# One batch's last transform stage with its products apart, and other steps for folds, stages and mixes in a fused FFT and channel-mix kernel

## The chip, the cores and the metric

The kernel runs on one core of one Trainium2 chip. The metric is the device time of an execution in microseconds. The kernel before the change took 428.42 us (median of 3 runs, 428.34 to 428.61).

The engines named below: PE multiplies matrices, ACT applies functions and copies, DVE does elementwise work, POOL issues the loads (and a few small operations), SP issues the stores. PE writes to PSUM alone, so each product is copied out by ACT or DVE ("evicted") before its PSUM buffer can be used again.

## The reference

```
# x: (8, 3072, 256); mu_k, mu_r: (256,); w_k: (256, 1024); w_v: (1024, 256); w_r: (256, 256)
X = np.fft.fft(x, axis=1)
X = np.fft.fft(X, axis=2)
x = X.real                                   # the mixed tokens

x_prev = concat([zeros, x[:, :-1, :]], axis=1)
xk = mu_k * x + (1.0 - mu_k) * x_prev
xr = mu_r * x + (1.0 - mu_r) * x_prev
k = np.maximum(xk @ w_k, 0.0)
v = k * k @ w_v
r = 1.0 / (1.0 + np.exp(-(xr @ w_r)))
out = r * v
```

First the real part of a two-dimensional Fourier transform over the sequence and the features of each batch, then a channel mix: a token shift with two weightings, a product with `w_k`, the square of its positive part, a product with `w_v`, and a gate.

## The kernel before, in words

**The channel mix sets the clock.** Each of the 8 batches has 6 chunks of 512 tokens (`m` says which half of the spectrum, `i` which third), 48 chunks in all, and each chunk has 4 steps. One step of the main loop does a K part (`k_piece`: 4 matmuls of 512 columns for two of the eight blocks of the hidden width, then the positive part on ACT into `rl`) and a v part (`v_tile`: 8 matmuls of 256 columns into a psV buffer, 5 steps behind the K part, `LAG`). Every fourth step has an r part (`r_item`: 8 matmuls, then a sigmoid on ACT). DVE squares `rl` into `k` two steps' worth at a time at odd steps (`square`, L845), and multiplies v by r into `o` at even steps (`v_out`, L888), which SP stores.

**The transform of later batches runs in between.** For batch `t` it goes through:

1. the load of two halves, plain (`xp`) and mirrored by an indirect gather (`xm`): `load_xh`, issued by POOL, behind `load_gate`, a tiny DVE write that POOL waits for, so that loads start at a chosen place in DVE's order;
2. `fold` (DVE, two adds) for each half, then `butterfly` (batches 1 and 2) or `quarters_1` and `quarters_2` (batch 3 on), all on DVE, into `eo`;
3. stage A: `a_item` or `a_half` (16 small matmuls per half and parity, evicted by ACT into `a`), with `a_slots_0` for two extra columns;
4. stage D: `d_item` (batches 1, 2) or `d_half` (from batch 3) into `g_all`, and `turned`, a matmul that fixes one column of `g_all` and writes it back;
5. the last stage, C, over 28 slots. `c_item` accumulates the cosine and the sine product in PSUM: two matmuls of 128 columns per slot, evicted straight into `y`. `c_pairs` keeps the two products apart: two matmuls of 64 columns per slot, evicted into `pq`, and DVE then adds and subtracts them into `y` (`halves`, L759, after one sign change at L756). The change finds batches 0 and 1 with `c_item` and the rest with `c_pairs`;
6. `diff` (DVE: differences of neighbouring slots, the token shift) and `mix(b, j, m, a)` (DVE, a scaling L779 and an add or subtract L790 into `x`). `j` is 0 for the K parts' operand and 1 for the r parts', `m` the half of the spectrum, `a` one of two operand halves. A matmul of a K part reads one `a`.

**What sets the order.** The order is written out by hand: `at(step, f, ...)` puts an item into a step, `event(step, ...)` groups several matmul items of the transform. In a step PE gets the K part, then the items of kind x, then the v part, then the event; DVE gets the x items' part, the event's, then the items of kind w and the product `o`, and last the square (in six steps named in `OUT_FIRST`, `o` comes ahead of the items). If the next step is in `early_v`, its v part follows directly behind the event. `event` puts the next step into `early_v` by itself where it has over two items and the first isn't `a_slots_0`. Every engine works through its own list in order.

**Buffers.** PSUM has three psW buffers in rotation, for K, r and all transform products, and two psV buffers. `p`, `t`, `y`, `pq`, `a`, `g_all`, `d` and each `x` exist once; `eo` twice; `xp` and `xm` three times.

**Batch and step.** Batch `b` has its K parts in steps 24b to 24b + 23. A batch's transform ends just before, so its steps are counted from s = 24t - 48 below.

The loop and the two order functions are in the part printed here; the lines that a sentence can't say:

```
for step in range(nk + LAG):
    if step < nk: k_piece(chunks[step // 4], step % 4)
    due(step, "x")
    v = v_steps.get(step)
    if v and step not in early_v: v_tile(*v)
    ...
    due(step, "e")
    if step + 1 in early_v:
        if step + 1 in v_steps: v_tile(*v_steps[step + 1])
    ...
    due(step, "w")
```

Of the kernel before, what the change touches and what calls it, by code (L numbers as in the profile page):

```python
# [39 lines left out]
def kernel(  # L40
# [12 lines left out]
    B, S, D = x.shape  # L53
# [52 lines left out]
    V = nc.vector  # L106
# [850 lines left out]
    for a in range(2):  # L957
        t = x_t["t", a] = mix_pool.tile([P, 24, 64], FP16, name=f"t{a}")
# [25 lines left out]
    def at(step, f, *args):  # L984
        work.setdefault((step, "x" if f in (a_item, a_sum, d_item, d_small, c_item, c_tiles, turned, minus_0, r_item, quarter_tables) else "w"),
                        []).append((f, args))
# [3 lines left out]
    early_v = set(range(17, 20))  # L990

    def event(step, *items):
        work.setdefault((step, "e"), []).extend((f[0], f[1:]) for f in items)
        if len(items) > 2 and items[0][0] is not a_slots_0:
            early_v.add(step + 1)

    chunks = [(b, m, i) for b in range(B) for m in range(2) for i in range(3)]
    nk = 4 * len(chunks)

    LAG, EARLY, SHORT = 5, 3, 3  # L1000
    EVENTS = (29, 33, 41, 45)
    OUT_FIRST = (12, 20, 28, 36, 38, 40)
    SQUARE_A = (6, 7, 8, 9)
    v_steps = {4 * n + tb + LAG: (c, tb) for n, c in enumerate(chunks) for tb in range(4)
# [23 lines left out]
    at(1, d_small, 0, 12, 1, "V")  # L1028
    at(2, mix_part, 0, 1, 0, 8)
    event(3, (half_tables,))  # L1030
    event(4, (c_item, 0, 17, 8))
    at(1, loads_1)
    at(4, loads_2)
# [26 lines left out]
    at(15, d_item, 1, 1, "V")  # L1060
    at(16, d_item, 1, 2, "A")
    at(16, d_item, 1, 3, "V")
    at(17, turned, 0, 13)
    at(17, r_item, (0, 1, 0))
    at(17, minus_0)
    at(17, c_tiles, 1)
    at(17, fold, 2, 0)
    event(18, (c_item, 1, 0, 8), (c_item, 1, 8, 8))
    at(18, butterfly, 2, 0)
    at(18, fold, 2, 1)  # L1070
    event(20, (c_item, 1, 16, 8), (c_item, 1, 24, 4), (a_half, 2, 0, 0))
    at(19, diff, 1, 0, 12)
    at(20, r_item, (0, 1, 1))
    at(23, a_half, 2, 0, 1)
    at(20, mix, 1, 0, 0, 0, 0, 12)
    at(21, butterfly, 2, 1)
    at(21, mix, 1, 0, 0, 1, 0, 12)
    at(22, diff, 1, 12, 26)
    at(21, load_gate)
    at(21, load_xh, 3, 1)  # L1080
    at(23, mix, 1, 0, 0, 0, 12, 24)
    at(24, r_item, (0, 1, 2))
    at(24, mix, 1, 1, 0, 0)
    at(24, mix, 1, 0, 0, 1, 12, 24)
    at(25, mix, 1, 1, 0, 1)
    at(26, mix, 1, 0, 1, 0)
    event(27, (a_slots_0, 2), (a_half, 2, 1, 0), (a_half, 2, 1, 1))
    at(28, r_item, (1, 0, 0))
    at(28, d_item, 2, 0)
    at(28, mix, 1, 0, 1, 1)  # L1090
    at(29, d_item, 2, 1)
    at(30, mix, 1, 1, 1, 0)
    at(31, d_item, 2, 2)
    at(31, mix, 1, 1, 1, 1)
    at(32, r_item, (1, 0, 1))
    at(33, d_item, 2, 3)
    at(34, turned, 0, 13)
    at(42, quarter_tables)
    for n, c in enumerate(chunks[8:]):
        at(4 * n + 36, r_item, c)  # L1100
    for b in range(B):
        s0 = 24 * b

        for n, st0 in enumerate((2, 4, 6, 8) if b > 1 else ()):
            at(s0 + st0, mix, b, n // 2, 1, n % 2)
        if b and b + 3 < B:
            at(s0 + 22, load_gate)
            for h in range(2):
                at(s0 + 22, load_xh, b + 3, h)
        t = b + 2  # L1110
        if t < B:
            if b:
                at(s0 + 9, fold, t, 0)
                at(s0 + 10, quarters_1, t, 0)
                at(s0 + 11, quarters_2, t, 0)
                at(s0 + 12, fold, t, 1)
                at(s0 + 14, quarters_1, t, 1)
                at(s0 + 15, quarters_2, t, 1)
            c = [(c_pairs, t, 8 * n, (8, 8, 8, 4)[n], "A") for n in range(4)]
            d = [(d_half, t, n) for n in range(4)]  # L1120
            a = [(a_half, t + 1, h, e) for h in range(2) for e in range(2)] if t + 1 < B else []
            if not b:
                event(s0 + 37, *c[:2], a[0])
                event(s0 + 41, *c[2:], a[1])
                event(s0 + 45, (a_slots_0, t + 1), *a[2:])
                continue
            at(s0 + 32, turned, 0, 12)
            at(s0 + 37, turned, 12, 13)
            event(s0 + EVENTS[0], *d[:3])
            early_v.add(s0 + EVENTS[0] + 2)  # L1130
            event(s0 + EVENTS[1], d[3], *c[:2])
            event(s0 + EVENTS[2], *c[2:], *a[:1])
            if a:
                event(s0 + EVENTS[3], (a_slots_0, t + 1), a[2], a[3], a[1])
                early_v.add(s0 + EVENTS[3] + 1)
        t = b + 1
        if b and t < B:
            at(s0 + 16, halves, t, 0, 15)
            at(s0 + 18, halves, t, 15, 27)
            for a in range(2):  # L1140
                at(s0 + 19 + a, diff, t, 0, 26, (a,))
                at(s0 + 21 + a, mix, t, 0, 0, a)
            at(s0 + 24, mix, t, 1, 0, 0)
            at(s0 + 25, mix, t, 1, 0, 1)

    def due(step, kind):
        for f, args in work.pop((step, kind), ()):
# [59 lines left out]
```

## Time and profile before

| | |
|---|---|
| median of 3 runs | 428.42 us |
| the profiled execution, whole | 428.89 us |
| its span, first to last instruction | 427.1 us |
| granted PE clock, mean over the span | 0.999 |
| DVE squares (L845, 2048 columns) | 88 of 1.22 us |
| ACT positive parts (L835) | 192 of 1.03 us |
| loads, issue to landing | 4.6 to 8.4 us |

The profile has views by engine, by line, of waits, of the chain of work that ended last, and a timeline. A timeline's row begins with the start and the length of a group in us; "x8" counts its instructions, and a bracket at the end gives idle time of the engine before it and what ended that. Matmuls overlap, so the time that a group of them takes is read from the start of the group to the start of the next, and not from its length.

### The profile page before, as it was taken

What the parts mean: (1) busy time and instruction counts of PE and PEld (TensorE: products, weight loads), DVE (VectorE), ACT (ScalarE), POOL (GpSimd) and SP (SyncE); (2) the same over time, 40 slices, a digit from 0 to 9 for tenths busy, and PEclk for the clock granted to TensorE, in tenths of its full rate; (3) what the DMA queues carried; (4) which work ended last, traced back from release to release, by engine and by line L of the source; (5) the groups of instructions that cost most, each with busy time, mean ns of one, the idle gap of its engine ahead of it and who ended that gap; (6) DMA issues with size and microseconds to landing.
All of it is one profiled execution on the core that took longest, in us unless ns stands there. A gap on an engine that the chain in (4) does not pass through costs nothing.

```text
span 427.1 us, 9641 instructions
## 1 busy us (share of the span) xinstructions
PE 421.1 (99%) x3991; PEld 295.3 (69%) x3991; DVE 367.8 (86%) x584; ACT 328.6 (77%) x409; POOL 62.3 (15%) x99
## 2 busy tenths in 40 slices
PE   8999999999999999999999999999999999999996
PEld 3767776777667777776777677767767776766765
DVE  8899999999897999979989899989999756997453
ACT  7889897878878878687786967778686877666661
POOL 7378502000050002300040000500000000000000
PEclk9999999999999999999999999999999999999999
DMA  8779967322286224932368222862232322323233
GB/s 172 108 108 188 231 142 131 75 56 69 61 151 157 55 58 82 194 86 57 79 116 179 67 58 67 144 152 61 64 75 51 75 68 58 73 63 71 66 75 99
DMA packets 35104, 42.08 MB, mean 99 GB/s; under 512 B 4114, under 2 KB 31092, under 8 KB 35060
## 3 DMA queue, kind: packets, MB, share of 16 engines
q1 hardware_dynamic: 27488, 25.41, 24.5%
q0 software_dynamic: 7264, 15.80, 22.1%
q8 instruction: 31, 0.51, 0.5%
q10 hardware_dynamic: 308, 0.26, 0.2%
q14 instruction: 13, 0.11, 0.1%
HBM read 32.08 MB, written 25.17 MB: 134 GB/s over the span
## 4 chain that ended last, share of the span: by engine, by line
PE 97%; ACT 1%; DVE 1%; issue 0%; POOL 0%; POOLq 0%
PE psW L825 39%; PE psV L866 37%; PE psW L852 10%; PE psV L878 3%; PE psW L746 1%; PE psW L617 1%; PE psW L235 1%; PE psW L679 1%; PE psW L635 1%; PE psW L657 1%; PE psW L714 1%; PE psV L378 1%; ACT pq L574 0%; DVE rw L308 0%; PE psV L657 0%
## 5 line engine op out<-in xcount | busy, mean ns | idle before, releaser
L835 ACT ACTIVATE rl<-psW 128x1024 f16<-128x1024 f32 x192 | 193.8, 1032 | 82.0 <-PE psW L825 77.1
L825 PE MATMUL psW<-x,wk 128*128 128x512 f16 (+1 forms) x776 | 193.6, 377 | 0.4 <-DVE x L962 0.3
L866 PE MATMUL psV<-wv_sb,k 128*128 128x256 f16 x1424 | 184.2, 273 | 0.0
L866 PEld LDWEIGHTS <-k 128*128 128x128 f16 x1424 | 136.5, 98 | 38.4
L845 DVE TENSOR_TENSOR k<-rl 128x2048 f16<-128x2048 f16 (+1 forms) x100 | 115.5, 1156 | 35.1 <-ACT rl L835 34.7
L825 PEld LDWEIGHTS <-wk 128*128 128x128 f16 x776 | 75.3, 98 | 55.1 <-issue 0.7
L888 DVE SCALAR_TENSOR_TENSOR o<-psV,r 128x512 f32<-128x512 f32 (+1 forms) x97 | 65.7, 680 | 12.2 <-PE psV L866 11.4
L790 DVE TENSOR_TENSOR x<-y,t 128x1536 f16<-128x1536 f16 (+3 forms) x74 | 62.0, 845 | 2.1
L857 ACT ACTIVATE r<-psW 128x1024 f16<-128x1024 f32 x48 | 49.5, 1032 | 0.8 <-PE psW L852 0.8
L852 PE MATMUL psW<-wr,x 128*128 128x256 f16 x384 | 49.8, 273 | 0.0
L852 PEld LDWEIGHTS <-x 128*128 128x128 f16 x384 | 37.5, 98 | 14.3
L574 ACT ACTIVATE g_all<-psW 128x512 f16<-128x512 f32 (+8 forms) x62 | 28.9, 540 | 1.3 <-PE psW L679 1.0
L574 ACT ACTIVATE a<-psW 128x832 f16<-128x832 f32 x31 | 25.7, 866 | 1.8 <-PE psW L617 1.4
L494 POOL IOTA gate<- 1x1 int32 x7 | 2.3, 323 | 158.8 <-DVE gate L493 158.8
L779 DVE TENSOR_SCALAR t<-d,muf_t 128x1536 f16<-128x1536 f16 (+3 forms) x42 | 21.9, 532 | 0.1
L574 ACT ACTIVATE pq<-psW 128x1024 f16<-128x1024 f32 (+1 forms) x24 | 20.8, 922 | 1.4 <-PE psW L746 1.4
L141 POOL DMA_INDIRECT xm<-in_x_dram,idx_g x18 | 20.9, 1164 | 5.5 <-issue 5.5
L172 DVE TENSOR_TENSOR p<-xp,xm 112x2304 f16<-112x2304 f16 (+6 forms) x19 | 21.6, 1139 | 0.0
L779 DVE TENSOR_SCALAR t<-d,mu_m 128x1536 f16<-128x1536 f16 x32 | 19.6, 613 | 0.0
L767 DVE TENSOR_TENSOR d<-y 128x1664 f16<-128x1664 f16 (+5 forms) x19 | 16.7, 879 | 0.2 <-ACT y L574 0.2
L759 DVE TENSOR_TENSOR y<-pq 128x960 f16<-128x960 f16 (+1 forms) x24 | 13.5, 605 | 2.0 <-ACT pq L574 1.8
L878 PE MATMUL psV<-wv_sb,k 128*128 128x256 f16 x112 | 14.7, 273 | 0.0
(149 smaller groups left out, 226.2 us busy)
## 6 DMA issues: line engine op xcount, KB each, us to landing
out_dram<-o SPq DMA_DIRECT2D x189, 128.0 KB, 2.4
xp<-in_x_dram POOLq DMA_DIRECT2D x12, 216.0 KB, 4.6
xp<-in_x_dram POOLq DMA_DIRECT2D x13, 192.0 KB, 7.5
xp<-in_x_dram POOLq DMA_DIRECT2D x2, 384.0 KB, 6.8
wv_sb<-in_moe_w_v_dram POOLq DMA_DIRECT2D x1, 512.0 KB, 8.4
xp<-in_x_dram SPq DMA_DIRECT2D x1, 480.0 KB, 4.2
xp<-in_x_dram POOLq DMA_DIRECT2D x1, 432.0 KB
xm<-in_x_dram,idx_g POOLq DMA_INDIRECT x18, 7.9
```

What stands on the lines that cost most here:

```text
L172: V.tensor_tensor(out=p[:, q0:q0 + n], in0=xp[:, q0:q0 + n], in1=_v(xm, o + 256, [(-256, n), (-1, 256)]), op=ALU.add)
L574: nc.scalar.activation(out=out_ap, in_=in_ap, func=AF.Copy)
L779: V.tensor_scalar(out=dst, in0=src, scalar1=mu, scalar2=None, op0=ALU.mult)
L790: V.tensor_tensor(out=_v(x_t[b, j, m], o, [(64 * step, hi - lo), (step, 64)]), in0=y_t[b][:, lo + 3 * m:hi + 3 * m, a], in1=x_t["t", a][:, ...
L825: nc.tensor.matmul(out=st["k", ds][:, 512 * hs + lo:512 * hs + hi], lhsT=wk_sb[m][a][:, 128 * fc:128 * fc + 128], rhs=xk[:, a, 512 * i + l ...
L835: nc.scalar.activation(out=st["rl"][:, 2 * ds:2 * ds + 2], in_=st["k", ds].rearrange("p (f t) -> p f t", f=2), func=AF.Relu, bias=0.0, sca ...
L845: V.tensor_tensor(out=k2_t[c][:, lo:hi], in0=r, in1=r, op=ALU.mult)
L852: nc.tensor.matmul(out=ps[:, 256 * tb:256 * tb + 256], lhsT=x_t[b, 1, m][:, a, 512 * i + 128 * tb: 512 * i + 128 * tb + 128], rhs=wr_sb[m] ...
L857: nc.scalar.activation(out=st["r", c], in_=ps, func=AF.Sigmoid)
L866: nc.tensor.matmul(out=st["v", tb - h][:, 256 * h:256 * h + 256], lhsT=k2_t[c][:, fc, 128 * tb:128 * tb + 128], rhs=wv_sb[:, fc], start=(f ...
L878: nc.tensor.matmul(out=st["v", tb - h][:, 256 * h:256 * h + 256], lhsT=k2_t[c][:, fc, 128 * tb:128 * tb + 128], rhs=wv_sb[:, fc], start=fc ...
L888: V.scalar_tensor_tensor(out=o.rearrange("p a b -> p (a b)")[:, 0:256 * n], in0=st["v", t0][:, 0:256 * n], scalar=16.0, in1=st["r", c][:, ...
```

## The change

The last stage of batch 1 goes from `c_item` to `c_pairs`, the first of its four groups evicted by DVE ("V"), the rest by ACT, with `halves` in two parts. `minus_0` and `c_tiles` go with it (`c_pairs` allocates `y` itself). Batch 2's second fold and butterfly go from steps 18 and 21 to 28 and 29, and its stage A from steps 20, 23 and 27 to 20 and 31, with the lone group of step 23 in the event of 31; its stage D starts at step 33 instead of 28. Batch 1's mixes are cut into more parts. The load of batch 3's second half goes from step 21 to 28, the quarter tables from 42 to 46. For the batches from 3 on, in steps from s: the quarters of the first half 12 and 13 instead of 10 and 11; the second half's fold 15 instead of 12, its quarters 26 and 27 instead of 14 and 15; the rest of stage A 29 instead of 21; stage D 33 and 37 instead of 29 and 33; `turned` 36 and 39 instead of 32 and 37; the mixes of the upper half of the spectrum 52, 54, 58 and 59 instead of 50, 52, 54 and 56. The differences, the mixes of the lower half and the loads stay at their steps. `early_v` is filled by a function `v_behind` and no longer by `event`.

```diff
     def event(step, *items):
         work.setdefault((step, "e"), []).extend((f[0], f[1:]) for f in items)
-        if len(items) > 2 and items[0][0] is not a_slots_0:
-            early_v.add(step + 1)
+
+    def v_behind(*steps):
+        early_v.update(steps)
...
+    at(17, r_item, (0, 1, 0))
     at(17, turned, 0, 13)
-    at(17, r_item, (0, 1, 0))
-    at(17, minus_0)
-    at(17, c_tiles, 1)
-    at(17, fold, 2, 0)
-    event(18, (c_item, 1, 0, 8), (c_item, 1, 8, 8))
-    at(18, butterfly, 2, 0)
-    at(18, fold, 2, 1)
-    event(20, (c_item, 1, 16, 8), (c_item, 1, 24, 4), (a_half, 2, 0, 0))
-    at(19, diff, 1, 0, 12)
-    at(20, r_item, (0, 1, 1))
-    at(23, a_half, 2, 0, 1)
-    at(20, mix, 1, 0, 0, 0, 0, 12)
-    at(21, butterfly, 2, 1)
+    at(16, fold, 2, 0)
+    at(17, butterfly, 2, 0)
+    event(18, (c_pairs, 1, 0, 8, "V"), (c_pairs, 1, 8, 8))
+    event(20, (c_pairs, 1, 16, 8), (c_pairs, 1, 24, 4), (a_half, 2, 0, 0))
+    v_behind(21)
+    at(19, halves, 1, 0, 13)
+    at(20, diff, 1, 0, 12)
+    at(21, r_item, (0, 1, 1))
+    at(21, mix, 1, 0, 0, 0, 0, 12)
     at(21, mix, 1, 0, 0, 1, 0, 12)
+    at(22, halves, 1, 13, 27)
     at(22, diff, 1, 12, 26)
-    at(21, load_gate)
-    at(21, load_xh, 3, 1)
+    at(28, load_gate)
+    at(28, load_xh, 3, 1)
...
-    event(27, (a_slots_0, 2), (a_half, 2, 1, 0), (a_half, 2, 1, 1))
+    at(28, fold, 2, 1)
+    at(29, butterfly, 2, 1)
+    event(31, (a_slots_0, 2), (a_half, 2, 1, 0), (a_half, 2, 1, 1), (a_half, 2, 0, 1))
+    v_behind(32)
...
-    at(42, quarter_tables)
+    event(39, (c_pairs, 2, 0, 8), (c_pairs, 2, 8, 8))
+    event(41, (c_pairs, 2, 16, 8), (c_pairs, 2, 24, 4), (a_half, 3, 0, 0))
+    v_behind(42)
...
+    at(46, quarter_tables)
...
+    for t in range(3, B):
+        s = 24 * t - 48
...
+        every(9, fold, 0)
+        every(12, quarters_1, 0)
+        every(13, quarters_2, 0)
+        every(15, fold, 1)
+        every(26, quarters_1, 1)
+        every(27, quarters_2, 1)
+        event(s + 29, (a_slots_0, t), (a_half, t, 1, 0), (a_half, t, 1, 1), (a_half, t, 0, 1))
+        event(s + 33, (d_half, t, 0), (d_half, t, 1), (d_half, t, 2))
+        at(s + 36, turned, 0, 12)
+        event(s + 37, (d_half, t, 3), (c_pairs, t, 0, 8), (c_pairs, t, 8, 8))
+        at(s + 39, turned, 12, 13)
+        event(s + 41, (c_pairs, t, 16, 8), (c_pairs, t, 24, 4),
+              *([(a_half, t + 1, 0, 0)] if t + 1 < B else ()))
+        v_behind(s + 30, s + 34, s + 35, s + 38, s + 42)
+        every(40, halves, 0, 15)
+        every(42, halves, 15, 27)
...
+        every(52, mix, 0, 1, 0)
+        every(54, mix, 0, 1, 1)
+        every(58, mix, 1, 1, 0)
+        every(59, mix, 1, 1, 1)
```

More of the change, by code (lines that the diff above doesn't have):

```diff
@@ L1000 @@
     LAG, EARLY, SHORT = 5, 3, 3
-    EVENTS = (29, 33, 41, 45)
     OUT_FIRST = (12, 20, 28, 36, 38, 40)
@@ L1081 @@
     at(23, mix, 1, 0, 0, 0, 12, 24)
     at(24, r_item, (0, 1, 2))
-    at(24, mix, 1, 1, 0, 0)
     at(24, mix, 1, 0, 0, 1, 12, 24)
-    at(25, mix, 1, 1, 0, 1)
-    at(26, mix, 1, 0, 1, 0)
-    event(27, (a_slots_0, 2), (a_half, 2, 1, 0), (a_half, 2, 1, 1))
-    at(28, r_item, (1, 0, 0))
[L1089 to L1094, printed above, removed]
-    at(32, r_item, (1, 0, 1))
-    at(33, d_item, 2, 3)
@@ L1097 @@
-    at(34, turned, 0, 13)
-    at(42, quarter_tables)
+    at(25, mix, 1, 1, 0, 0, 0, 12)
+    at(26, mix, 1, 1, 0, 1, 0, 12)
+    at(27, mix, 1, 1, 0, 0, 12, 24)
+    at(30, mix, 1, 1, 0, 1, 12, 24)
+    at(28, fold, 2, 1)
+    at(29, butterfly, 2, 1)
+    event(31, (a_slots_0, 2), (a_half, 2, 1, 0), (a_half, 2, 1, 1), (a_half, 2, 0, 1))
+    v_behind(32)
+    at(28, r_item, (1, 0, 0))
+    at(33, d_item, 2, 0)
+    at(34, d_item, 2, 1)
+    at(31, mix, 1, 0, 1, 0)
+    at(32, mix, 1, 0, 1, 1)
@@ new lines @@
+    at(34, mix, 1, 1, 1, 0)
+    at(35, d_item, 2, 2)
+    at(35, mix, 1, 1, 1, 1)
+    at(32, r_item, (1, 0, 1))
+    at(36, d_item, 2, 3)
+    at(37, turned, 0, 13)
+    event(39, (c_pairs, 2, 0, 8), (c_pairs, 2, 8, 8))
+    event(41, (c_pairs, 2, 16, 8), (c_pairs, 2, 24, 4), (a_half, 3, 0, 0))
+    v_behind(42)
+    at(41, halves, 2, 0, 15)
+    at(42, halves, 2, 15, 27)
+    at(43, diff, 2, 0, 26, (0,))
+    at(44, diff, 2, 0, 26, (1,))
+    at(45, mix, 2, 0, 0, 0)
+    at(46, mix, 2, 0, 0, 1)
@@ L1099 @@
+    at(48, mix, 2, 1, 0, 0)
+    at(49, mix, 2, 1, 0, 1)
+    at(52, mix, 2, 0, 1, 0)
+    at(54, mix, 2, 0, 1, 1)
+    at(58, mix, 2, 1, 1, 0)
+    at(59, mix, 2, 1, 1, 1)
+    at(46, quarter_tables)
     for n, c in enumerate(chunks[8:]):
         at(4 * n + 36, r_item, c)
[L1101 to L1144, printed above, removed]
@@ new lines, with every @@
+    for t in range(3, B):
+        s = 24 * t - 48
+        def every(step, f, *args):
+            at(s + step, f, t, *args)
+        every(9, fold, 0)
[14 more added lines that the diff above has]
+        every(42, halves, 15, 27)
+        every(43, diff, 0, 26, (0,))
+        every(44, diff, 0, 26, (1,))
+        every(45, mix, 0, 0, 0)
+        every(46, mix, 0, 0, 1)
+        every(48, mix, 1, 0, 0)
+        every(49, mix, 1, 0, 1)
+        every(52, mix, 0, 1, 0)
+        every(54, mix, 0, 1, 1)
+        every(58, mix, 1, 1, 0)
+        every(59, mix, 1, 1, 1)
@@ L1146, in due @@
+    for b in range(4, B):
+        at(24 * b - 50, load_gate)
+        for h in range(2):
+            at(24 * b - 50, load_xh, b, h)
     def due(step, kind):
```

## Prediction, made before the change was run

> **What bounds the kernel now.** I read the page first: the busy shares and the chain that ended last.
>
> ```profile
> PE 421.1 (99%) x3991; PEld 295.3 (69%) x3991; DVE 367.8 (86%) x584; ACT 328.6 (77%) x409; POOL 62.3 (15%) x99
> ...
> PE 97%; ACT 1%; DVE 1%; issue 0%; POOL 0%; POOLq 0%
> ```
>
> A busy matmul engine alone proves little, since matmuls overlap in the records. So next the waits: which waits of PE end on another engine?
>
> ```profile
> DVE k L845 <- ACT rl L835: 34.7, 30, 2.1
> ...
> PE psW L235 <- DVE xm L266: 1.0, 1, 1.0
> ...
> PE psW L825 <- DVE x L962: 0.3, 1, 0.3
> ```
>
> PE's longest own waits are these two, both in the start-up that the change leaves alone. The squares on DVE wait 34.7 us for ACT, so DVE catches up with its inputs again and again. PE sets the end, and its program can become shorter only by PE work that goes, or by a gap that the records hide. It becomes longer where a moved step lets DVE or ACT be late. So I read PE's timeline for what each touched event takes, then the margins of what PE waits for.
>
> The unit is a step: a K part (4 matmuls, 0.87) and a v part (8 matmuls, 0.87), with an r part (0.87) every fourth step. What an event costs is the time between the starts around it, less 0.87 for the group that starts it.
>
> **What goes.** PE in the stretch of batch 1's last stage (L714), and the lone group of batch 2's stage A (L617):
>
> ```profile
> 55.68 1.03 PE L825 MATMUL psW<-x,wk 128*128 128x512 f16 x4
> ...
> 57.64 1.05 PE L866 MATMUL psV<-wv_sb,k 128*128 128x256 f16 x8
> ...
> 61.12 1.04 PE L866 MATMUL psV<-wv_sb,k 128*128 128x256 f16 x8
> 62.09 0.84 PE L714 MATMUL psW<-m_cs,g_all 64*128 64x128 f16 x24
> ...
> 63.07 1.05 PE L866 MATMUL psV<-wv_sb,k 128*128 128x256 f16 x8
> ...
> 67.42 1.04 PE L866 MATMUL psV<-wv_sb,k 128*128 128x256 f16 x8
> 68.38 0.37 PE L617 MATMUL psW<-w_hh,eo 48*128 48x52 f16 x16
> 68.69 1.04 PE L825 MATMUL psW<-x,wk 128*128 128x512 f16 x4
> ```
>
> Event of step 18, two products groups: 57.64 - 55.68 - 0.87 = 1.09. Event of step 20, two groups and one A: 63.07 - 61.12 - 0.87 = 1.08. The lone A of step 23: 68.69 - 67.42 - 0.87 = 0.40.
>
> The form that takes their place (cosine and sine apart, L746, 64 columns instead of 128) already runs for batch 2:
>
> ```profile
> 97.78 1.04 PE L866 MATMUL psV<-wv_sb,k 128*128 128x256 f16 x8
> 98.75 0.64 PE L746 MATMUL psW<-m_cs,g_all 64*128 64x64 f16 x32
> 99.22 0.36 PE L617 MATMUL psW<-w_hh,eo 48*128 48x52 f16 x16
> 99.52 1.05 PE L866 MATMUL psV<-wv_sb,k 128*128 128x256 f16 x8
> ...
> 106.48 1.04 PE L866 MATMUL psV<-wv_sb,k 128*128 128x256 f16 x8
> ...
> 108.10 1.05 PE L866 MATMUL psV<-wv_sb,k 128*128 128x256 f16 x8
> ```
>
> From the end of the v part (98.65) to 99.22 are 0.57: 32 matmuls in 0.47, and 0.10 of entry into the half-height form. With 0.10 to leave it again, two groups alone cost 0.67. The event with 24 and one A costs 108.10 - 106.48 - 0.87 = 0.75. So step 18 saves 1.09 - 0.67 = **0.42**, step 20 saves 1.08 - 0.75 = **0.33**.
>
> Here a rule of the Trainium skill speaks against the change: "TensorE: Matmul & The Clock Gate", section "Wait — 56ns, not 53.3ns?", says that start-to-start never drops below about 25 ns, however few the columns. By it the 56 matmuls would take an estimated 1.4 us, with their entries and exits 1.8, and these two savings together would be about 0.2 instead of 0.75, the time 427.7. The trace disagrees: 32 in 0.47 us are 15 ns each, with the two halves of the array in turn, and the sum goes by the trace.
>
> The lone A joins the event of step 31, where three A groups run at once, as they already do from batch 4 on:
>
> ```profile
> 115.42 1.04 PE L866 MATMUL psV<-wv_sb,k 128*128 128x256 f16 x8
> ...
> 116.95 1.04 PE L825 MATMUL psW<-x,wk 128*128 128x512 f16 x4
> ...
> 264.29 1.04 PE L866 MATMUL psV<-wv_sb,k 128*128 128x256 f16 x8
> 265.16 1.03 PE L825 MATMUL psW<-x,wk 128*128 128x512 f16 x4
> 266.02 1.04 PE L866 MATMUL psV<-wv_sb,k 128*128 128x256 f16 x8
> ...
> 267.05 0.77 PE L617 MATMUL psW<-w_hh,eo 48*128 48x52 f16 x46
> 267.75 1.05 PE L866 MATMUL psV<-wv_sb,k 128*128 128x256 f16 x8
> ...
> 271.23 1.03 PE L825 MATMUL psW<-x,wk 128*128 128x512 f16 x4
> ```
>
> Two A groups with their slots: 116.95 - 115.42 - 0.87 = 0.66. Three: 267.75 - 266.02 - 0.87 = 0.86. The third costs 0.20 in company and 0.40 alone: **0.20** saved.
>
> The quarter tables hold a gap that the waits do not name:
>
> ```profile
> 109.29 0.87 ACT L574 ACTIVATE a<-psW 128x832 f16<-128x832 f32 x1
> ...
> 109.85 0.22 PE L551 MATMUL psW<-w_eo,same 128*128 128x128 f16 x1
> ...
> 110.22 1.02 PE L825 MATMUL psW<-x,wk 128*128 128x512 f16 x4
> ```
>
> The matmul needs a quarter of a K matmul (0.87 / 4 / 4 = 0.05), but the next K starts 0.37 later: right after the A eviction ends (109.29 + 0.87 = 110.16), which frees the third psW buffer. The table's tile had taken the one that was free. At step 46 no event is near, and the K of step 43 takes the free buffer: 0.37 - 0.05 = **0.31** saved (rounded down).
>
> Sum: 0.42 + 0.33 + 0.20 + 0.31 = 1.26.
>
> **What moves, and what it is hidden by.** From batch 3 on the same events run with the same neighbours, only at other steps: three A groups four steps after the batch before starts its K work (step 5 of 24 instead of 21), the D groups at 9 and 13 instead of 5 and 9. As many entries into the half-height form, so no PE work is gained or lost. ACT's evictions now come in every group of four steps from 5 to 17:
>
> ```profile
> 291.49 1.02 ACT L835 ACTIVATE rl<-psW 128x1024 f16<-128x1024 f32 x1 [0.41 <-PE psW L825]
> ```
>
> That is the fourth step after the heaviest event (six D evictions, begun after the v part of 282.53, shown below): ACT is idle again 8.5 us later, before the next event's evictions. The A event moved ahead of it has three, so ACT carries nothing over, and I count nothing.
>
> What can cost is DVE. Three margins are the tightest; their rows:
>
> ```profile
> 50.95 1.22 DVE L572 CAST g_all<-psW 128x1024 f16<-128x1024 f32 x1 [0.25 <-PE psW L657]
> ...
> 252.59 1.36 DVE L183 TENSOR_TENSOR t<-p 112x1024 f16<-112x1024 f16 x3
> ...
> 255.89 1.22 DVE L845 TENSOR_TENSOR k<-rl 128x2048 f16<-128x2048 f16 x1
> ...
> 265.36 0.69 DVE L888 SCALAR_TENSOR_TENSOR o<-psV,r 128x512 f32<-128x512 f32 x1 [0.21 <-PE psV L866]
> ...
> 266.22 1.02 ACT L835 ACTIVATE rl<-psW 128x1024 f16<-128x1024 f32 x1 [0.67 <-PE psW L825]
> ...
> 269.29 0.96 DVE L790 TENSOR_TENSOR x<-y,t 128x1536 f16<-128x1536 f16 x1
> ...
> 276.71 1.22 DVE L845 TENSOR_TENSOR k<-rl 128x2048 f16<-128x2048 f16 x1
> ...
> 282.53 1.04 PE L866 MATMUL psV<-wv_sb,k 128*128 128x256 f16 x8
> ```
>
> - *The next batch's first K (six times, batches 2 to 7).* DVE's chain starts when PE's v part of step 20 (264.29) releases the output product (265.36), and ends with the second half of x at 269.29 + 0.96 = 270.25; the K of step 24 starts at 271.23. The A event (0.86) between them goes away, so K comes at 270.37. Its second matmul is the first that reads this half, 0.22 later: 270.59. Margin 0.34, where 1.20 stood. Behind it stands everything on PE. DVE's chain itself has the same instructions in the same order.
> - *The square of step 3 (five times, batches 2 to 6).* Before it DVE now does the second half's quarters instead of one mix. The square of step 1 ends 277.93; quarters with the output product between them take 255.89 - 252.59 = 3.30; the square 1.22: 282.45. The v part at 282.53 reads the first half of the hidden columns for 0.44, then this square: 282.97. Margin 0.5.
> - *Batch 1's fill.* DVE gets one eviction (1.22, like the 50.95 row) and four halves more, and gives back a fold and butterfly of two operations each to steps 28 and 29. K of step 19 now starts near 58.1. From a K's start to its rectification's end are 266.22 + 1.02 - 265.16 = 2.08: 60.2, the square ends 61.4. PE reads it from 58.1 + 1.74 + 0.87 + 0.75 + 0.44 = 61.9. Margin 0.5, once. In the same event A's buffer is that of step 20's K, rectified at 58.1 + 0.87 + 2.08 = 61.05, and A comes at 58.1 + 1.74 + 0.87 + 0.10 + 0.47 x 24/32 = 61.16: 0.1 of margin, and 0.1 or so of price if it is missed.
>
> So I take nothing for waits. The bounds: above, each margin missed by as much as it is wide (0.34 six times is 2.0, and 0.5 five times 2.5); below, nothing, since no wait beyond the one at 110.22 is there to remove.
>
> The load of batch 3's second half goes on POOL's queue seven steps later, behind nothing else there, and has eleven steps until its fold at step 39:
>
> ```profile
> xm<-in_x_dram,idx_g POOLq DMA_INDIRECT x18, 7.9
> ```
>
> Eleven steps are at least 11 x 1.74 = 19 us against 7.9 to landing and a few to issue: hidden. In the later batches POOL's loads stay at the same step.
>
> **The sum.** Profiled span 427.1 - 1.26 = 425.8. The profiled execution took 428.89 with what lies around its span, the median of the runs is 428.42; I take the difference off the median: 428.42 - 1.26 = **427.2**.
>
> **The rivals.**
> 1. *x comes late.* Some tenths of DVE delay (POOL's descriptor work at step 22, a longer semaphore path) use up 0.34 and leave 0.1 six times: 0.6 back, 427.8. For it: the smallest margin, repeated. Against it: the same chain took 265.36 to 270.25 with those loads in it.
> 2. *Slower: the same wait, larger.* If DVE enters step 20 behind, its 0.21 of idle at 265.36 is used up first, then the 0.34. With a delay of 1.0 per batch K waits 0.45 six times, 2.7: 427.2 + 2.7 = 429.9. It decides from a delay of 0.9 on (six times 0.35 is the 2.1 that turns the gain into a loss of 0.2%). For it: DVE is at 86%, and halves now follow a fold at step 15. Against: that fold (1.4) replaces quarters that ended as late (255.89), and the square that follows them waits for ACT anyway.
> 3. *The squares of step 3 come late*, by 0.2 five times: 1.0 back, 428.2. Against: 0.5 of margin.
> 4. *The products gain nothing.* If the two halves of the array did not take turns where these groups stand alone (step 18), a 64-column matmul would take an eighth of a K matmul's 0.217, 0.027, and L714's took (63.07 - 62.09 - 0.30) / 24 = 0.028 with 128 columns. Of the 0.75 some 0.7 is gone: 427.9. Against: the 98.75 row. The floor of the Trainium skill, named above, would come to much the same.
>
> **How the numbers follow.** Forecast 0.56, rivals 1 to 4: 0.18, 0.13, 0.08, 0.05. A difference under 0.2% (0.86 us) is about what can't be told from none. Faster by more means under 427.56: the forecast and a quarter of rival 1, 0.60. Slower by more, over 429.28: 0.13. Same: 0.27. The range reaches from a gain of 1.6 (the terms read 0.1 low each) to rival 3's side of no change: 426.8 to 428.5; the forecast alone has 426.9 to 427.5.
>
> **What would show it.** L714 leaves the stretch from 50 us on; L746 has 56 more matmuls, with the events near 56.6 and 60.8 taking 0.67 and 0.75. No lone L617 group of 16. The K after L551 starts 0.05 to 0.1 after it. K of step 24 near 67.5, and the period of a late batch unchanged. Rivals 1 and 2 would show as PE waiting for DVE x at L825, and a longer period; rival 3 as PEld L866 waiting for DVE k at a period's third square. I am wrong if the span of 130 to 420 us changes by more than 0.3: then DVE was not as far ahead as these rows say.

## The result, and the profile after

| | before | after |
|---|---|---|
| median of 8 runs each, on the same chip | 428.53 us (428.34 to 430.20) | 427.26 us (427.19 to 427.62) |
| after / before | | 0.9966, 95% interval 0.9954 to 0.9977 |
| the profiled execution, and its span | 428.89, 427.1 us | 427.19, 425.4 us |

The change gains 1.27 us by the medians; the forecast was 1.26. The ratio goes by the means of the runs (427.34 over 428.79), and its interval reaches from a gain of 1.0 us to one of 2.0: that the medians agree with the forecast to 0.01 is luck. First the page of the kernel after: the busy time of each engine in us with its share of the span, and the shares of the chain of work that ended last.

```profile
PE 419.5 (99%) x3991; PEld 294.6 (69%) x3991; DVE 371.4 (87%) x593; ACT 327.2 (77%) x407; POOL 64.3 (15%) x99
...
PE 98%; DVE 1%; issue 0%; POOL 0%; ACT 0%; POOLq 0%
```

PE has as many matmuls as before, and fewer us of them. DVE does 3.6 us more than before and the kernel is faster: DVE's busy time does not set the end. The waits of the kernel after (who waits for whom: us in total, times, longest) tell the same:

```profile
DVE k L845 <- ACT rl L835: 26.0, 27, 2.1
...
PE psW L235 <- DVE xm L266: 1.0, 1, 1.0
```

DVE's spare time in front of the squares went from 34.7 to 26.0 us, and PE's longest wait is still the one in the start-up. The view names no new wait of PE. So the gain must lie in PE's own list, and PE's timeline of the kernel after (start, length, engine, line, operation, count) shows where:

```profile
50.66 1.03 PE L825 MATMUL psW<-x,wk 128*128 128x512 f16 x4
...
55.15 1.03 PE L825 MATMUL psW<-x,wk 128*128 128x512 f16 x4
56.11 0.64 PE L746 MATMUL psW<-m_cs,g_all 64*128 64x64 f16 x32
56.68 1.05 PE L866 MATMUL psV<-wv_sb,k 128*128 128x256 f16 x8
...
59.29 1.04 PE L866 MATMUL psV<-wv_sb,k 128*128 128x256 f16 x8
...
60.93 1.05 PE L866 MATMUL psV<-wv_sb,k 128*128 128x256 f16 x8
...
67.02 1.03 PE L825 MATMUL psW<-x,wk 128*128 128x512 f16 x4
...
81.79 1.04 PE L866 MATMUL psV<-wv_sb,k 128*128 128x256 f16 x8
...
83.52 1.05 PE L866 MATMUL psV<-wv_sb,k 128*128 128x256 f16 x8
...
115.19 0.22 PE L551 MATMUL psW<-w_eo,same 128*128 128x128 f16 x1
115.25 0.93 PE L866 MATMUL psV<-wv_sb,k 128*128 128x256 f16 x7
...
268.66 1.03 PE L825 MATMUL psW<-x,wk 128*128 128x512 f16 x4
...
279.95 1.04 PE L866 MATMUL psV<-wv_sb,k 128*128 128x256 f16 x8
```

| term | before | forecast | after, from start to start | saved |
|---|---|---|---|---|
| event of step 18 | 1.09 | 0.67 | 56.68 - 55.15 - 0.87 = 0.66 | 0.43 |
| event of step 20 | 1.08 | 0.75 | 60.93 - 59.29 - 0.87 = 0.77 | 0.31 |
| lone A of step 23 | 0.40 | 0.20 in company | event of step 31: 83.52 - 81.79 - 0.87 = 0.86, where two A groups took 0.66 | 0.20 |
| quarter tables | 0.37 | 0.05 | 115.25 - 115.19 = 0.06 | 0.31 |
| sum | | 1.26 | | **1.25** |

Behind the tables' matmul stands a v part at step 46, and not the K that the prediction named as the sign; the K behind that v part is not late.

The spans of the two profiled executions differ by 1.7. The K at 50.66 is that of step 16, the last ahead of the stretch that was changed, and 0.52 of the 1.7 is gone before it (before, that K started at 51.18), where nothing was changed on PE's list. From that K to the end are 374.7 instead of 375.9 us: 1.2. The rest belongs to the two executions, and the medians do not have it. From the K of step 24 (67.02, 68.69 before) to the end, with all the late batches, are 358.4 us in both, where 0.1 less was due (0.20 for the third A group, 0.31 for the gap). PE's timeline of the kernel after shows where that 0.1 went:

```profile
101.31 1.04 PE L825 MATMUL psW<-x,wk 128*128 128x512 f16 x4
102.27 1.03 PE L852 MATMUL psW<-wr,x 128*128 128x256 f16 x8
```

This is step 40, behind the event of step 39 with two groups of products of batch 2. The r part starts 0.96 behind the K instead of 0.87: it takes the psW buffer of the first group, and ACT's eviction of that group, begun at 101.19, takes 1.02, to 102.21. The wait has no row in the view of waits. So PE's list is shorter by 1.25 - 0.09 = 1.16, which is the 1.2 of the two profiles.

Now the margins, read against the K at 268.66 and the v part at 279.95 of the timeline above. The timeline of DVE of the kernel after, in batch 1's fill and around the start of a late batch:

```profile
59.73 1.22 DVE L845 TENSOR_TENSOR k<-rl 128x2048 f16<-128x2048 f16 x1
...
267.56 0.96 DVE L790 TENSOR_TENSOR x<-y,t 128x1536 f16<-128x1536 f16 x1
...
278.34 1.22 DVE L845 TENSOR_TENSOR k<-rl 128x2048 f16<-128x2048 f16 x1
```

- The second half of x ends at 267.56 + 0.96 = 268.52, and the K's second matmul, the first to read it, starts at 268.66 + 0.22 = 268.88: margin 0.36 (forecast 0.34).
- The square of step 3 ends at 279.56. The v part reads it from its fifth matmul on, at 279.95 + 0.44 = 280.39: margin 0.83 (forecast 0.5).
- In the fill, the square ends at 60.95, and the v part of 60.93 needs it at 61.37: margin 0.42 (forecast 0.5).

### The profile page after: what moved, and what is told of

Its sections match the earlier page's. It is cut to its first block, busy times and chain, and to the rows that moved or that the text cites. A ratio compares the mean times of both kernels' runs of the same rounds, so it can differ in the third digit from the quotient of the medians.

```text
span 425.4 us, 9649 instructions
## 1 busy us (share of the span) xinstructions
PE 419.5 (99%) x3991; PEld 294.6 (69%) x3991; DVE 371.4 (87%) x593; ACT 327.2 (77%) x407; POOL 64.3 (15%) x99
## 4 chain that ended last, share of the span: by engine, by line
PE 98%; DVE 1%; issue 0%; POOL 0%; ACT 0%; POOLq 0%
PE psW L825 39%; PE psV L866 37%; PE psW L852 10%; PE psV L878 3%; PE psW L746 2%; PE psW L617 1%; PE psW L679 1%; PE psW L235 1%; PE psW L635 1%; PE psW L657 1%; PE psV L378 1%; PE psW L714 0%; DVE rw L308 0%; PE psV L657 0%; PE psV L635 0%
## 5 line engine op out<-in xcount | busy, mean ns | idle before, releaser
L494 POOL IOTA gate<- 1x1 int32 x7 | 0.8, 121 | 163.8 <-DVE gate L493 163.8
L574 ACT ACTIVATE pq<-psW 128x1024 f16<-128x1024 f32 (+1 forms) x27 | 23.3, 917 | 1.5 <-PE psW L746 1.4
L141 POOL DMA_INDIRECT xm<-in_x_dram,idx_g x18 | 23.5, 1304 | 5.5 <-issue 5.5
L759 DVE TENSOR_TENSOR y<-pq 128x960 f16<-128x960 f16 (+3 forms) x28 | 15.8, 604 | 3.2 <-ACT pq L574 2.8
```

What stands on the lines that cost most here:

```text
L141: nc.gpsimd.indirect_dma_start(dst, None, src, bass.IndirectOffsetOnAxis(ap=idx, axis=0))
L574: nc.scalar.activation(out=out_ap, in_=in_ap, func=AF.Copy)
```

## The experiments

The kernels were timed in three groups, each on one chip beside its own runs of the kernel before (medians 428.45, 428.47 and 428.72). The 95% intervals of the ratios are about 1 us wide, so where a term of some tenths is in question the profile decides, and the times say whether they contradict it. "Lost" is against the median of the kernel after, 427.26, which is from another chip; the kernel before moved by up to 0.3 between the groups.

**The four terms, undone one at a time.** In the first kernel, batch 1's last stage adds up in PSUM again:

```
+    at(17, minus_0)
+    at(17, c_tiles, 1)
-    event(18, (c_pairs, 1, 0, 8, "V"), (c_pairs, 1, 8, 8))
-    event(20, (c_pairs, 1, 16, 8), (c_pairs, 1, 24, 4), (a_half, 2, 0, 0))
+    event(18, (c_item, 1, 0, 8), (c_item, 1, 8, 8))
+    event(20, (c_item, 1, 16, 8), (c_item, 1, 24, 4), (a_half, 2, 0, 0))
-    at(19, halves, 1, 0, 13)
-    at(22, halves, 1, 13, 27)
```

> The changed kernel with batch 1's last stage back as accumulated products. My theory (PE's list alone sets the time): the events of steps 18 and 20 take 1.09 and 1.08 us again instead of 0.66 and 0.77, so 0.74 us of the gain of 1.27 is lost: about 0.5 us faster than before. Rival (the gain comes from the later steps of the batches from 3 on, or from less DVE work at the wrong time): this kernel, which keeps those steps and spares DVE the halves, is as fast as the changed one or faster, 1.2 us or more under before.

Measured: 428.06 (ratio to before 0.9990, 0.9981 to 0.9999), 0.80 lost. PE's timeline of this kernel:

```profile
55.33 1.03 PE L825 MATMUL psW<-x,wk 128*128 128x512 f16 x4
...
57.33 1.05 PE L866 MATMUL psV<-wv_sb,k 128*128 128x256 f16 x8
...
59.94 1.04 PE L866 MATMUL psV<-wv_sb,k 128*128 128x256 f16 x8
...
61.88 1.05 PE L866 MATMUL psV<-wv_sb,k 128*128 128x256 f16 x8
```

The events are 57.33 - 55.33 - 0.87 = 1.13 and 61.88 - 59.94 - 0.87 = 1.07 long again, 0.77 more than after's 0.66 and 0.77. The span of this execution is no measure of the edit: the D items of step 16, ahead of all that the edit touches, took 0.77 in it and 0.56 in the kernel after, and between 0.55 and 1.05 in the other profiles.

Next, the lone A group goes back to step 23:

```
-    event(31, (a_slots_0, 2), (a_half, 2, 1, 0), (a_half, 2, 1, 1), (a_half, 2, 0, 1))
+    event(31, (a_slots_0, 2), (a_half, 2, 1, 0), (a_half, 2, 1, 1))
+    at(23, a_half, 2, 0, 1)
```

> The changed kernel with one group of batch 2's stage A alone in step 23 again. My theory: it costs 0.40 us alone and 0.20 in company, so 0.20 us of the gain is lost, read from PE's timeline as 0.40 in step 23 and 0.66 in the event of step 31; the medians show about 1.05 us under before. Rival (entering and leaving the half-height form is hidden elsewhere): no change in the span.

Measured: 427.48 (0.9973, 0.9963 to 0.9984), 0.22 lost. PE's timeline of this kernel:

```profile
66.73 1.04 PE L866 MATMUL psV<-wv_sb,k 128*128 128x256 f16 x8
67.69 0.37 PE L617 MATMUL psW<-w_hh,eo 48*128 48x52 f16 x16
68.00 1.04 PE L825 MATMUL psW<-x,wk 128*128 128x512 f16 x4
```

Alone it costs 68.00 - 66.73 - 0.87 = 0.40, as in the kernel before, and the event of step 31 takes 84.31 - 82.78 - 0.87 = 0.66 in this kernel; the loss of 0.22 is what the group costs more than the 0.20 in company.

Then the quarter tables go back to step 42, `at(42, quarter_tables)` for `at(46, ...)`, and as a counterpart only this edit is put into the kernel before:

> The changed kernel with the quarter tables at step 42 again. My theory: the matmul takes the free psW buffer and the K of step 43 waits for the A eviction, 0.3 us; the start of that K comes 0.37 after the table's matmul instead of 0.06, and about 0.95 us under before remain. Rival (the gap of before came from the weight load of another shape and not from the buffer): 0.06 to 0.1 at step 42 too, no change.

> The kernel before with the quarter tables alone moved to step 46. My theory: 0.3 us under before, PE's start after the table's matmul 0.06 later instead of 0.37. Rival (the gap only moves to another K, since the A event of step 45 takes the buffers there): no change, a gap near step 46 or 47.

Measured: with step 42 in the kernel after, 427.53 (0.9975, 0.9964 to 0.9985), 0.27 lost; with step 46 in the kernel before, 428.40 (0.9995, 0.9986 to 1.0004), 0.32 gained by the medians. The timeline of the first, ACT and then PE:

```profile
107.81 0.87 ACT L574 ACTIVATE a<-psW 128x832 f16<-128x832 f32 x1
```

```profile
108.37 0.22 PE L551 MATMUL psW<-w_eo,same 128*128 128x128 f16 x1
108.74 1.02 PE L825 MATMUL psW<-x,wk 128*128 128x512 f16 x4
```

In the second, the matmul starts at 117.41 and the v part behind it at 117.46. The gap is 0.37 at step 42 and 0.05 or 0.06 at step 46 in either kernel. What it waits for is argued: the K at step 42 starts 0.06 after the end of the A eviction (107.81 + 0.87 = 108.68), as in the kernel before (110.16 and 110.22), and in the rotation of the three psW buffers it comes to the one that A had. Since a v part, and no K, stands behind the matmul at step 46, the move alone doesn't rule out that a K behind this matmul is slow whatever the buffer. The second ratio's interval holds 1, so the gain from the tables alone is shown by the trace and not by that timing.

The three edits lose 0.80 + 0.22 + 0.27 = 1.29 together. (Taken from the gains over the kernel before in the same group, 0.39, 0.97 and 0.92 where the change has 1.27, they lose 0.88, 0.30 and 0.35, or 1.53: each is good to about 0.1.) By either sum that is the whole gain.

**The products apart without the moves around them.** The kernel before gets the two events of `c_pairs` and the two `halves`, and keeps every other step:

```
-    at(17, minus_0)
-    at(17, c_tiles, 1)
-    event(18, (c_item, 1, 0, 8), (c_item, 1, 8, 8))
+    event(18, (c_pairs, 1, 0, 8, "V"), (c_pairs, 1, 8, 8))
-    event(20, (c_item, 1, 16, 8), (c_item, 1, 24, 4), (a_half, 2, 0, 0))
+    event(20, (c_pairs, 1, 16, 8), (c_pairs, 1, 24, 4), (a_half, 2, 0, 0))
+    at(19, halves, 1, 0, 13)
+    at(22, halves, 1, 13, 27)
```

> The kernel before with batch 1's products apart and nothing else moved (halves at steps 19 and 22). PE's list gets 0.74 us shorter. My theory: DVE gets 2.3 us (an eviction, a sign, two halves) ahead of the square of step 19, which ended at 62.2 with PE's v part at 63.07 and its fifth matmul at 63.5; it now ends near 64.4 with that matmul due at 62.8, so PE waits 1.6 there, and the time is 0.5 to 1.5 us above before: the fold and butterfly had to go first. Rival (DVE's idle 0.8 before 55.60 takes it up): 0.7 us under before.

Measured: 431.17 (1.0062, 1.0049 to 1.0076), 2.45 slower than before, where the interval has 2.1 to 3.3. The direction was expected, the size was not: the expectation had one wait of 1.6. DVE's timeline of this kernel:

```profile
58.13 1.42 DVE L211 TENSOR_TENSOR eo<-p 112x1152 f16<-112x1152 f16 x2
59.46 1.22 DVE L172 TENSOR_TENSOR p<-xp,xm 112x2048 f16<-112x2048 f16 x1
...
61.69 1.09 DVE L759 TENSOR_TENSOR y<-pq 128x832 f16<-128x832 f16 x2
...
63.70 1.22 DVE L845 TENSOR_TENSOR k<-rl 128x2048 f16<-128x2048 f16 x1
```

and PE's:

```profile
62.27 0.61 PE L866 MATMUL psV<-wv_sb,k 128*128 128x256 f16 x4
64.97 0.61 PE L866 MATMUL psV<-wv_sb,k 128*128 128x256 f16 x4 [2.09 <-DVE k L845]
...
73.64 0.60 PE L866 MATMUL psV<-wv_sb,k 128*128 128x256 f16 x4
74.62 0.61 PE L866 MATMUL psV<-wv_sb,k 128*128 128x256 f16 x4 [0.38 <-DVE k L845]
```

DVE has the butterfly, the second fold, the halves and the differences ahead of one square, and the second half of the v part waits for it. The second four matmuls should follow 0.44 behind the first, and come 64.97 - 62.27 - 0.44 = 2.26 and 74.62 - 73.64 - 0.44 = 0.54 later than that. Less the 0.75 that the events save this is 2.05, and the profiled span grew by 2.1. So without the other moves the 0.75 of the products apart turns into a loss. By DVE's rows the second fold of batch 2 and the butterflies, which the change moves, are in the way; they were not moved alone, so this part is argued.

**The later batches' steps.** First, the old steps for the quarters, the second fold, stages A and D, `turned` and the mixes of batches 4 to 7 only:

```
+        o = t > 3
...
-        every(12, quarters_1, 0)
-        every(13, quarters_2, 0)
-        every(15, fold, 1)
...
+        every(10 if o else 12, quarters_1, 0)
+        every(11 if o else 13, quarters_2, 0)
+        every(12 if o else 15, fold, 1)
...
+        e_a, e_d = (s + 21, s + 29) if o else (s + 29, s + 33)
...
+        for n in range(4):
+            every((50, 52, 54, 56)[n] if o else (52, 54, 58, 59)[n], mix, n // 2, 1, n % 2)
```

> The changed kernel with the batches from 4 on at the steps of before. My theory: PE waits for nothing in either order, so nothing changes: 1.2 to 1.3 us under before, the period of a late batch equal in both to 0.05 us. Rival (the later steps are worth something by themselves): the time goes back towards before by 0.4 us or more.

Measured: 430.11 (1.0033, 1.0021 to 1.0045), 2.85 lost: the expectation was wrong. PE's timeline of this kernel has the place:

```profile
147.14 0.60 PE L866 MATMUL psV<-wv_sb,k 128*128 128x256 f16 x4
148.83 0.61 PE L866 MATMUL psV<-wv_sb,k 128*128 128x256 f16 x4 [1.09 <-DVE k L845]
```

Its waits, and DVE's timeline ahead of that square:

```profile
PE psV L866 <- DVE k L845: 2.4, 2, 1.3
```

```profile
140.93 0.61 DVE L779 TENSOR_SCALAR t<-d,mu_m 128x1536 f16<-128x1536 f16 x1
...
142.46 1.50 DVE L183 TENSOR_TENSOR t<-p 112x1152 f16<-112x1152 f16 x3
...
144.47 0.61 DVE L779 TENSOR_SCALAR t<-d,mu_m 128x1536 f16<-128x1536 f16 x1
...
147.56 1.22 DVE L845 TENSOR_TENSOR k<-rl 128x2048 f16<-128x2048 f16 x1
```

The edit mixed two schedules. Batch 2's last mixes stayed at steps 58 and 59, and batch 4's quarters went back to the same two steps (s = 48, 10 and 11); batches 3 and 5 meet likewise at 82 and 83. Both stand ahead of one square, which the second half of a v part needs: 148.83 - 147.14 - 0.44 = 1.25 of PE, and once more a batch later, 201.29 - 199.44 - 0.44 = 1.41. The following batches, with both at the old steps, show no such wait. To separate the collision from the steps themselves, the next kernel has the same old steps with the old mix steps for all batches, and batch 2's last mixes at 55 and 56:

```
-    at(58, mix, 2, 1, 1, 0)
-    at(59, mix, 2, 1, 1, 1)
+    at(55, mix, 2, 1, 1, 0)
+    at(56, mix, 2, 1, 1, 1)
...
+        for n in range(4):
+            every((50, 52, 54, 56)[n], mix, n // 2, 1, n % 2)
```

> The batches from 4 on at the steps of before once more, now with the upper mixes of batch 2 at 52, 54, 55, 56 and of batch 3 at the steps of before, so that no two mixes stand between a quarters pass and the square of step 11. My theory (old4 lost 2.8 us to two waits of PE for that square alone, 1.3 and 1.4, both where moved mixes met unmoved quarters; the steps themselves are worth nothing): no such wait, 1.1 to 1.3 us under before. Rival (the old steps cost something in every batch): 0.4 us or more above the changed kernel.

Measured: 427.42 (0.9973, 0.9962 to 0.9983), 0.16 from the kernel after and no more than the runs scatter; no wait of a v part on k. Against the kernel before in its own group it gains 1.30. The later batches' new steps are worth nothing by themselves, as the prediction counted them, but they belong together.

**The margin of x.** A DVE write that nobody reads is put ahead of the last mix before each of the batches 2 to 7, in two sizes (it only adds work):

```
+    pad = const.tile([P, 1024], INT32)
+    def late(n):
+        V.memset(pad[:, 0:n], 0)
...
+    for b in range(2, B):
+        at(24 * b - 2, late, 300)
```

> The changed kernel with an extra DVE write of about 0.3 us ahead of the last mix before each batch from 2 to 7 (six times). The output is the same. My theory (x has 0.34 us of margin at the next batch's first K): the delay fits into the margin, nothing is lost, 1.2 to 1.3 us under before. Rival (the margin is already used up by paths that the profile does not show): 0.2 us and more each time, over 1.2 us in all, no gain over before is left.

> The same with a DVE write of about 1.0 us. My theory: x is late by 1.0 - 0.34 = 0.66 us six times, 4.0 us more than the changed kernel, about 2.7 us over before; PE shows as many waits of L825 for DVE x, and all of it stays, since nothing on PE can be made up. Rival (PE's weight loads run ahead and the loss is caught up in the same batch, or the delay moves other things too): clearly less than 3 us or more than 5.

Measured with 300: 427.38 (0.9973, 0.9963 to 0.9983), nothing lost. With 1000: 431.09 (1.0061, 1.0047 to 1.0074), 3.83 lost. DVE's timeline of the smaller size:

```profile
266.98 0.31 DVE L985 MEMSET pad<- 128x300 int32 x1
...
267.74 0.96 DVE L790 TENSOR_TENSOR x<-y,t 128x1536 f16<-128x1536 f16 x1
```

and PE's:

```profile
268.63 1.03 PE L825 MATMUL psW<-x,wk 128*128 128x512 f16 x4
```

x ends at 268.70, and the K's second matmul starts at 268.63 + 0.22 = 268.85: 0.15 of the 0.36 is left, so the write of 0.31 delayed x by 0.21 only. The larger size, DVE and then PE:

```profile
268.96 0.89 DVE L985 MEMSET pad<- 128x1000 int32 x1 [0.16 <-issue]
...
270.30 0.96 DVE L790 TENSOR_TENSOR x<-y,t 128x1536 f16<-128x1536 f16 x1
```

```profile
270.46 0.38 PE L825 MATMUL psW<-x,wk 128*128 128x512 f16 x1
271.31 0.81 PE L825 MATMUL psW<-x,wk 128*128 128x512 f16 x3 [0.47 <-DVE gate L493]
```

x ends at 271.26; K's second matmul should start at 270.68 and starts at 271.31, 0.63 late. The other five waits are 0.57 (before batch 2) and four of 0.63: 3.7 in all, of 3.83 measured. The delay, counted against PE, is 0.94 (x ended 0.14 ahead of the K's start, and now 0.80 behind it): 0.94 less the margin of 0.36, and 0.05 from the end of the write to the matmul. The row names the tiny write of `load_gate` as the releaser; that write stands behind x on DVE, and the matmul reads x. Before batches 6 and 7, where no such write stands, the same wait of 0.47 is put down to x itself.

**The margin of the square of step 3.** The larger write at step 3 of the batches 2 to 6:

```
+    for b in range(2, B - 1):
+        at(24 * b + 3, late, 1000)
```

> The changed kernel with a DVE write of about 1.0 us at step 3 of the batches 2 to 6 (five times), ahead of the square there. I predicted 0.5 us of margin for this square; the profile after shows 279.56 for its end against 280.39 for the fifth matmul of the v part, 0.8. By the first, five waits of 0.5, 2.5 us lost; by the second, five waits of 0.2, 1.0 us lost. If neither holds (the next square waits for ACT, and v parts have more room), nothing is lost.

Measured: 428.43 (0.9998, 0.9989 to 1.0007), 1.17 lost. The timeline, PE and then DVE:

```profile
280.61 1.27 PE L866 MATMUL psV<-wv_sb,k 128*128 128x256 f16 x8
281.71 0.21 PE L603 MATMUL psW<-w_hh,eo 112*128 112x52 f16 x2
```

```profile
279.99 1.22 DVE L845 TENSOR_TENSOR k<-rl 128x2048 f16<-128x2048 f16 x1
```

The v part takes 281.71 - 280.61 = 1.10 instead of 0.87: 0.23 lost. The five places lose 0.22, 0.23, 0.24, 0.23 and 0.15, together 1.07. The square ends at 281.21, and the fifth matmul was due at 280.61 + 0.44 = 281.05: with 0.05 from the end of the write to the matmul that is 0.21 of the 0.23. From 0.83 ahead to 0.16 behind, the write delayed the square by 0.99. With the margin of 0.5 that the prediction had, 0.99 - 0.5 + 0.05 = 0.54 would have been lost each time.

**One product more apart.** If batch 1's products gain 0.74, does a group of batch 0 gain too? (`c_pairs` also gets a tile `pq` for batch 0 and a start at an odd slot.)

```
-    event(4, (c_item, 0, 17, 8))
+    event(4, (c_pairs, 0, 17, 8))
+    at(5, halves, 0, 17, 25)
```

> A step beyond the change: slots 17 to 24 of batch 0's last stage with the products apart too (16 matmuls of 64 columns instead of 128, evicted by ACT, two more adds on DVE). My theory: PE's event of step 4 takes 0.2 us less, and about 1.45 us under before if DVE's two adds (0.8 us) still leave x in time for the third chunk. Rival (DVE is the bound in the start-up): PE waits for x at step 8, and the time is that of the changed kernel or 0.5 us worse.

Measured: 427.45 (0.9977, 0.9968 to 0.9986), no gain over the kernel after (0.19 more): the expectation was wrong. PE's event does become shorter. PE's timeline of this kernel, where lines from 746 on are one higher:

```profile
24.72 1.04 PE L879 MATMUL psV<-wv_sb,k 128*128 128x256 f16 x8
...
26.03 1.04 PE L826 MATMUL psW<-x,wk 128*128 128x512 f16 x4
...
31.64 1.20 PE L879 MATMUL psV<-wv_sb,k 128*128 128x256 f16 x8
```

The event is 26.03 - 24.72 - 0.87 = 0.44 long, 0.21 less than in the kernel after. But the v part at 31.64 is 1.20 long instead of the usual 1.04, and the one at 40.39 is 1.19. In the kernel after, DVE had waited 0.50 for PE ahead of the output products at 30.40; with the halves it comes to them at 30.91 without a wait, later than PE needs their psV buffers. From the K's start ahead of each of these two v parts to the start of the K behind it are 1.96 (30.71 to 32.67) and 2.66 (38.76 to 41.42), against 1.74 and 2.45 in the kernel after: 0.43 lost for 0.21 gained. No kernel that was tried is faster than the changed one.

## Why the prediction was right

- *PE's list alone sets the time.* Right. The four terms sum to 1.25 in the profile after (1.26 forecast), and the terms undone one by one lose 1.29 together, or 1.53 by the second way. Each term was read to 0.01 or 0.02; the times alone would allow 1.0 to 2.0.
- *The products apart: 0.42 + 0.33.* Right: 0.43 and 0.31. The 0.02 missing in the event of step 20 is not the A's buffer, for which 0.1 of margin was seen: A starts 0.36 behind the products (60.26 to 60.62), as at batch 2 in the kernel before (107.45 to 107.81). The 32 matmuls of 64 columns start at 56.11 and the v part behind them at 56.68: less the 0.10 to leave the half-height form, 15 ns each. The floor of the Trainium skill ("TensorE: Matmul & The Clock Gate", section "Wait — 56ns, not 53.3ns?") would give an estimated 32 x 25 = 0.80 us; the trace doesn't agree, and rival 4 falls with it.
- *The lone A, 0.20, and the quarter tables, 0.31.* Right in size, both in the kernel after and undone; that the gap is a wait for A's buffer fits its rows and is not shown apart. It has no row in the waits of the kernel before; it came from reading start to start.
- *Nothing for waits.* Right but for 0.09. "From batch 3 on the same events run with the same neighbours" doesn't hold for batch 3: its stage A stood in the events of steps 37, 41 and 45 (one, one and two groups) and now stands in 41 and 53 (one and three). The events themselves cost the same, 0.87 + 0.75 + 0.66 = 2.28 before and 0.67 + 0.76 + 0.86 = 2.29 now, but behind the two groups of products that now stand alone the r part of step 40 waits 0.09 for its buffer. The margin that mattered most was right in size: 0.34 forecast, 0.36 read. A DVE write that delayed x by 0.21 cost nothing, one that delayed it by 0.94 cost six waits of about 0.6. So the mechanism of rivals 1 and 2 exists, and the size of the waits fits a threshold at the margin of 0.36; its condition wasn't met. Rival 2 put the delay at which the gain turns into a loss at 0.9, since 0.21 of idle ahead of the chain was to be used up first. The written delay came behind that idle time and had only the 0.36 against it.
- *The square of step 3 (rival 3).* Not late. Its margin was mis-sized: 0.83, not 0.5. The prediction had the square of step 1 end 282.53 - 277.93 = 4.60 ahead of the v part, and it ends (at 273.91 + 1.22 = 275.13) 279.95 - 275.13 = 4.82 ahead; and it gave the work from there through the square 3.30 + 1.22 = 4.52, which took 279.56 - 275.13 = 4.43, since the quarters start at 275.04, 0.09 ahead of the recorded end of the square before them.
- *The stretch from 130 us on.* Unchanged, as said: from the K at 268.66 to the end are 156.7 us, and from the same K before (271.23) 155.9, with the event of 0.86 now behind this K.

What the prediction did not see is what the moves are for. It costed them as hidden, which is so, but treated them as independent. The products apart with everything else at the old steps lose 2.45; by the rows it is batch 2's second fold and the butterflies that have to be out of the way. The old quarters beside the late mixes lose 2.85. Each time several DVE operations too many stood ahead of one square. For the batches from 4 on the moves bring nothing: with all old steps there the time is the same.

## What to carry to other kernels

When one engine's list sets the end, price a change by start-to-start times on that engine, from the nearest place where the same form already runs, and look for gaps that the view of waits doesn't name. Then give each buffer or operand that the engine reads its margin from the slack of whoever writes it, and count how often it recurs: here a delay of 0.94 us against a margin of 0.36, six times, turned a gain of 1.3 into a loss of 2.6. Work that moves off a crowded place is part of the price of what moves in; test the two together and apart.

## What the runs showed of the hardware

- From the end of a DVE write to the start of the matmul that waits for it were 0.05 us, for x (271.26 to 271.31) and for k (64.92 to 64.97, 74.57 to 74.62 and 148.78 to 148.83 in the kernels whose v parts wait).
- Entering the half-height form cost 0.09 us: the lone A starts at 67.69, and the v part ahead of it has its 0.87 by 67.60. From 67.69 to the K at 68.00 are 0.31, and the group takes 0.20 in company, so leaving it cost 0.11, an estimate. By it, half of what a lone group costs is the change of form.
- A DVE write's recorded length is not what it delays: 0.31 us of write moved what follows by 0.21, while 0.89 us moved it by 0.94 and by 0.99, with 0.16 of issue ahead of it.
